# Rotating scan states out in the last phase instead of in the scan pass, with a new head for the x loads

## The chip, the cores and the metric

The kernel runs on one core of a Trainium2 chip. The metric is the device time of one execution in microseconds (us), lower is better. PE is TensorE, DVE is VectorE, ACT is ScalarE, POOL is GpSimd and SP is SyncE; SP computes nothing here and issues nearly all DMAs.

## The reference

With x of 2048 rows (time) by 1024 columns in bf16, two branches are computed and mixed by a gate per row:

```
g = sigmoid((x * gate_w).sum(-1))
a = irfft2(rfft2(x) * (w_r + 1j*w_i))                  # over both axes, to bf16

Lam = Lambda_re + 1j*Lambda_im                         # 1024 complex states
Lam_bar = exp(exp(log_dt) * Lam)
Bu[t] = x[t] @ (((Lam_bar - 1) / Lam)[:, None] * (B_re + 1j*B_im)).T
h[t] = Lam_bar * h[t-1] + Bu[t]
b[t] = 2 * real(h[t] @ (C_re + 1j*C_im).T) + x[t] * Dskip

out = g * a + (1 - g) * b
```

## The kernel before

**Scan branch.** The 1024 states are 8 blocks `jb` of 128 partitions, the 2048 times 4 chunks `c` of `TC` = 512. `pass1(jb)` does one block: PE multiplies x transposed (`xT`) with the block of B (64 matmuls, L296), ACT casts the result to `u` (L299), and DVE takes the phase out of the recurrence, so that a real scan is left: it rotates the input (`cu`, `su`, `v`, L301 to L305, by rows 0 to 2 of the table `tab`), runs two scans per chunk into `g` (L308), computes the carry to the next chunk (L313 to L317), and rotates the output into `h` (`cu`, `su`, `h`, L320 to L324, by rows 3 to 5 of `tab`). Three DVE operations of 128 x 1024 elements each do such an output rotation; it is called a trio below. `h` goes to DRAM, into `h_dram[c]` (L325). ACT and DVE build `tab` once per block (L275 to L289); its two buffers alternate.

**Fourier branch.** `gfnet()` is a generator; `pull(budget)` runs pieces of it between the passes. It transforms along columns (`fd`, matmuls L334, cast into `X` on ACT L337) and along time in two steps (L346 to L349, then, after a corner turn through DRAM, load `Bb` L434 and matmuls L440), multiplies by W on DVE (`Wr_b`, `Wi_b`, L447 to L452), and goes back the same way (L464, turn, `Cq` L485, L488, `ps_id` L506, gated into `ga` L511). `T3_sb` (`T_sb` in the profile) and `K3_sb` hold the transforms along time. Two columns of W need a repair of their own (`fixup`), for which `Wc` takes four columns of W element by element (L358 to L361).

**Phase B.** When all blocks are done, for each chunk `hch` (2 MB) is loaded from `h_dram[c]` (L542), PE multiplies it with C (`CT`, 128 matmuls a chunk, L550), and DVE forms the skip term `sk`, `pre` and the output `o` for each of four row blocks (L558, L560, L563).

**The head.** For 16 row blocks of x: load into one of three staging buffers `xn` (L157), transpose on PE, copy into `xT` (L147), and sum x times `gate_w` on DVE (`gjunk`, L159). The C blocks go through the same staging buffers later, from L265, into `CT`.

**Order.** The framework sorts the program for each engine by a cost model of its own, and each engine then runs its list strictly in order. Tiles of a pool wait for a free buffer. A DMA queue's issuing engine is held while an instruction in front of it waits.

Of the kernel before, what the change touches and what calls it, by code (L numbers as in the profile page):

```python
# [14 lines left out]
BF16 = mybir.dt.bfloat16  # L15
I32 = mybir.dt.int32
# [65 lines left out]
def kernel(  # L82
# [60 lines left out]
    def pe_transpose_block(src_ap, dst_ap, evac):  # L143
        pt = psU.tile([P, 8, P], BF16, name="pt", tag="psu")
        for j8 in range(8):
            nc.tensor.transpose(out=pt[:, j8, :], in_=src_ap[:, P * j8:P * (j8 + 1)], identity=ident)  # L146
        evac(out=dst_ap, in_=pt)  # L147

    xT = xpool.tile([P, 8, S], BF16, name="xT")
# [4 lines left out]
    gjunk = cpool.tile([P, D], BF16, name="gjunk")  # L154
    for r in range(16):
        xn = stg.tile([P, D], BF16, name="xn", tag="stg")
        nc.sync.dma_start(out=xn, in_=x[P * r:P * (r + 1), :])  # L157
        pe_transpose_block(xn, xT[:, :, P * r:P * (r + 1)], nc.vector.tensor_copy)
        nc.vector.scalar_tensor_tensor(out=gjunk, in0=xn, scalar=1.0, in1=gw_bc, op0=ALU.mult, op1=ALU.mult,  # L159
                                       accum_out=glog[:, r:r + 1])  # L160

# [94 lines left out]
    tau_i = cpool.tile([P, TC], I32, name="tau_i")  # L256
# [3 lines left out]
    CT = [ctpool.tile([P, 8, D], BF16, name=f"CT{ri}") for ri in range(2)]  # L260

    def load_CT_block(ri, q):
        src = (B_C_re, B_C_im)[ri]
        cn = stg.tile([P, D], BF16, name="cn", tag="stg")
        nc.sync.dma_start(out=cn, in_=src[P * q:P * (q + 1), :])  # L265
        pe_transpose_block(cn, CT[ri][:, :, P * q:P * (q + 1)], nc.scalar.copy)

    def pass1(jb):
        BTs = p1.tile([P, 2, 8, P], BF16, name="BTs")
        for ri, src in enumerate((B_B_re, B_B_im)):  # L270
# [16 lines left out]
        nc.scalar.mul(out=tab[:, 4, :], in_=tab[:, 3, :], mul=-1.0)  # L287
        nc.vector.scalar_tensor_tensor(out=tab[:, 5, :], in0=sn_f, scalar=ncr[:, jb:jb + 1], in1=t2,
                                       op0=ALU.mult, op1=ALU.subtract)  # L289
        rb = r_sb[:, jb:jb + 1].to_broadcast([P, TC])  # L290
        carry = None
        for c in range(NCH):
            psu = psU.tile([P, 2, TC], FP32, name="psu", tag="psu")
            for ri in range(2):
                for dblk in range(8):
                    nc.tensor.matmul(psu[:, ri, :], lhsT=BTs[:, ri, dblk, :], rhs=xT[:, dblk, TC * c:TC * (c + 1)],  # L296
                                     start=(dblk == 0), stop=(dblk == 7))
# [7 lines left out]
            nc.vector.tensor_add(out=v, in0=cu, in1=su)  # L305
            g = rp.tile([P, 2, TC], BF16, name="g")
            for ri in range(2):
                nc.vector.tensor_tensor_scan(out=g[:, ri, :], data0=rb, data1=v[:, ri, :],  # L308
                                             initial=(0.0 if carry is None else carry[:, ri:ri + 1]),
                                             op0=ALU.mult, op1=ALU.add)  # L310
# [8 lines left out]
            cg = rp.tile([P, 2, TC], BF16, name="cu")  # L319
            nc.vector.tensor_mul(out=cg, in0=g, in1=tab[:, 3:5, :])  # L320
            sg = rp.tile([P, 2, TC], BF16, name="su")
            nc.vector.tensor_mul(out=sg, in0=g[:, ::-1, :], in1=tab[:, 5:6, :].to_broadcast([P, 2, TC]))  # L322
            h = hp.tile([P, 2, TC], BF16, name="h")
            nc.vector.tensor_add(out=h, in0=cg, in1=sg)  # L324
            nc.sync.dma_start(out=h_dram[c, :, jb, :, :], in_=h)  # L325

    def gfnet():
        Acol = fx.tile([P, 16, 2], BF16, name="Acol")
# [26 lines left out]

        Wc = fx.tile([P, 16, 4], BF16, name="Wc")
        with nc.allow_non_contiguous_dma(reason="two columns of W"):
            nc.sync.dma_start(out=Wc[:, :, 0], in_=Wr_v[:, :, 0])  # L358
            nc.sync.dma_start(out=Wc[:, :, 1], in_=Wi_v[:, :, 0])  # L359
            nc.sync.dma_start(out=Wc[:, :, 2], in_=Wr_v[:, :, K])  # L360
            nc.sync.dma_start(out=Wc[:, :, 3], in_=Wi_v[:, :, K])  # L361
# [70 lines left out]
        def s2w(b):  # L432
# [95 lines left out]
    for jb in range(8):  # L528
# [2 lines left out]
            load_CT_block(*ct_blocks.pop(0))  # L531
        pull(24.0)
    pull(1e9)
    actx.close()
    with ExitStack() as bctx:
        hcp = bctx.enter_context(tc.tile_pool(name="hcp", bufs=2))
        fin = bctx.enter_context(tc.tile_pool(name="fin", bufs=2))
        psY = bctx.enter_context(tc.tile_pool(name="psY", bufs=3, space=PSUM))

        for c in range(NCH):  # L540
            hch = hcp.tile([P, 8, 2, TC], BF16, name="hch")
            nc.sync.dma_start(out=hch, in_=h_dram[c])  # L542
# [53 lines left out]
```

## Time and profile before

| | |
|---|---|
| four runs | 539.31 us median, 538.5 to 541.11 |
| profiled execution | 539.43 us, its span 537.7 us |
| mean granted TensorE clock | 0.958 |
| PE busy | 443.2 us, 82% of the span, 2343 matmuls |
| DVE busy | 355.8 us, 66% |
| ACT busy | 211.3 us, 39% |
| POOL busy | 8.3 us, 2% |
| DMA | 74.18 MB, mean 138 GB/s |

A row of the timeline gives the start, the length, the engine, the line of the kernel and the operation, output<-inputs, the shapes, how many instructions were merged, and in brackets the idle time of that engine just before, with what ended it. SPq is SP's queue of DMA instructions. A row of the stage table gives a stretch and its length, the busy time of PE, PEld (weight loads, beside PE), DVE, ACT and POOL with instruction counts, then granted clock, the DMA engines' share and GB/s. For a DMA issue the last number is the time from issue to landing.

### The profile page before, as it was taken

How to read it: one execution, taken by the hardware profiler on the slowest of the kernel's cores; microseconds unless marked ns; L12 is line 12 of the kernel's file. 1: busy time of each engine (PE TensorE's matmuls, PEld its weight loads, DVE VectorE, ACT ScalarE, POOL GpSimd, SP SyncE). 2: the span in 40 equal slices, each digit the busy share in tenths (PEclk: the TensorE clock that was granted, in tenths of full speed). 3: DMA queues.
4: the chain of work that ended last, by engine and by line, in shares of the span. 5: the costliest groups of instructions: out<-in, count | busy, mean ns of one | idle time of the engine just before them, and what ended most of it. 6: DMA issues, size and time to landing. Idle time of an engine off the chain costs nothing.

```text
span 537.7 us, 6325 instructions
## 1 busy us (share of the span) xinstructions
PE 443.2 (82%) x2343; PEld 224.9 (42%) x2343; DVE 355.8 (66%) x633; ACT 211.3 (39%) x278; POOL 8.3 (2%) x16
## 2 busy tenths in 40 slices
PE   2045998989969956899977999999890799999996
PEld 1033544544635522443433545554440344444442
DVE  4069459937940996999999990505979944444431
ACT  0000596685456345657784755653521000000000
POOL 4000000000000010000000000000000000000000
PEclk9999999899979996989998999999996699999999
DMA  9974222311412198748765343520255646555211
GB/s 205 190 175 124 54 80 77 120 59 41 125 51 79 60 208 206 212 131 265 234 195 123 126 144 119 174 102 20 99 184 206 256 135 216 176 197 195 78 40 40
DMA packets 59519, 74.18 MB, mean 138 GB/s; under 512 B 21600, under 2 KB 32096, under 8 KB 58976
## 3 DMA queue, kind: packets, MB, share of 16 engines
q1 hardware_dynamic: 54016, 69.28, 40.8%
q0 software_dynamic: 5136, 3.97, 4.8%
q10 hardware_dynamic: 336, 0.53, 0.5%
q8 instruction: 18, 0.29, 0.2%
q14 instruction: 13, 0.11, 0.1%
HBM read 52.53 MB, written 25.19 MB: 145 GB/s over the span
## 4 chain that ended last, share of the span: by engine, by line
PE 36%; DVE 34%; DMA 10%; ACT 8%; issue 6%; SPq 5%; DVEq 0%
PE ps_y L550 21%; DVE g L308 10%; PE ps_fd L334 4%; PE ps_id L506 4%; DVE cu L301 3%; DVE v L305 3%; DVE su L303 3%; DVE su L322 3%; PE psu L296 3%; DVE h L324 2%; DMA xn<-in_A_x_dram 2%; SPq L359 2%; DMA Wi_b<-in_A_w_i_dram 2%; DMA Bb<-turn_scratch 2%; DMA hch<-h_scratch 1%
## 5 line engine op out<-in xcount | busy, mean ns | idle before, releaser
L550 PE MATMUL ps_y<-CT,hch 128*128 128x512 bf16 x512 | 113.1, 385 | 15.6 <-DMA hch<-h_scratch 15.6
L296 PE MATMUL psu<-xT,BTs 128*128 128x512 bf16 x512 | 119.6, 382 | 3.2 <-ACT BTs L147 3.0
L550 PEld LDWEIGHTS <-hch 128*128 128x128 bf16 x512 | 50.5, 99 | 77.9 <-DMA hch<-h_scratch 15.7
L296 PEld LDWEIGHTS <-BTs 128*128 128x128 bf16 x512 | 49.8, 98 | 61.9 <-ACT BTs L147 4.0
L334 PE MATMUL ps_fd<-G_sb,xT 128*128 128x512 bf16 x256 | 64.8, 410 | 10.4 <-ACT X L337 9.7
L506 PE MATMUL ps_id<-Ginv_sb,ZT 128*128 128x512 bf16 x256 | 58.5, 383 | 1.7 <-ACT ga L511 1.6
L308 DVE TENSOR_TENSOR_SCAN g<-r_sb,carry,v 128x512 bf16<-128x512 f32 x48 | 59.1, 1271 | 0.5
L301 DVE TENSOR_TENSOR cu<-u,tab 128x1024 bf16<-128x1024 bf16 x32 | 22.0, 686 | 56.3 <-ACT u L299 56.1
L563 DVE SCALAR_TENSOR_TENSOR o<-ps_y,omg,pre 128x1024 bf16<-128x1024 f32 x16 | 20.5, 1284 | 57.3 <-PE ps_y L550 57.3
L334 PEld LDWEIGHTS <-xT 128*128 128x128 bf16 x256 | 37.0, 147 | 34.1 <-issue 19.1
L299 ACT CAST u<-psu 128x1024 bf16<-128x1024 f32 x32 | 32.4, 1012 | 46.7 <-PE psu L296 39.8
L146 PE MATMUL pt<-ident,xn 128*128 128x128 bf16 x128 | 16.2, 311 | 37.9 <-DMA xn<-in_A_x_dram 34.4
L506 PEld LDWEIGHTS <-ZT 128*128 128x128 bf16 x256 | 25.2, 98 | 32.6 <-issue 5.3
L159 DVE SCALAR_TENSOR_TENSOR gjunk<-xn,gw_bc 128x1024 bf16<-128x1024 bf16 x16 | 19.5, 1219 | 22.5 <-DMA xn<-in_A_x_dram 17.1
L146 PEld LDWEIGHTS <-xn 128*128 128x128 bf16 x128 | 12.5, 141 | 41.4 <-DMA xn<-in_A_x_dram 39.2
L511 ACT ACTIVATE ga<-ps_id,gA 128x1024 bf16<-128x1024 f32 x16 | 17.8, 1110 | 28.3 <-issue 14.2
L337 ACT CAST X<-ps_fd 128x1024 bf16<-128x1024 f32 x16 | 16.1, 1005 | 19.9 <-PE ps_fd L334 19.9
L305 DVE TENSOR_TENSOR v<-cu,su 128x1024 bf16<-128x1024 bf16 x32 | 22.1, 689 | 0.7
L320 DVE TENSOR_TENSOR cu<-g,tab 128x1024 bf16<-128x1024 bf16 x32 | 22.0, 687 | 0.2
L324 DVE TENSOR_TENSOR h<-cu,su 128x1024 bf16<-128x1024 bf16 x32 | 22.0, 687 | 0.2
L469 ACT CAST C<-ps_is 128x1024 bf16<-128x1024 f32 x16 | 16.3, 1017 | 14.5 <-PE ps_is L467 8.0
L303 DVE TENSOR_TENSOR su<-u,tab 128x1024 bf16<-128x1024 bf16 x32 | 21.9, 686 | 0.0
(185 smaller groups left out, 532.9 us busy)
## 6 DMA issues: line engine op xcount, KB each, us to landing
h_scratch<-h SPq DMA_DIRECT2D x32, 256.0 KB, 2.1
hch<-h_scratch SPq DMA_DIRECT2D x4, 2048.0 KB, 7.9
xn<-in_A_x_dram SPq DMA_DIRECT2D x16, 256.0 KB, 3.7
turn_scratch<-A SPq DMA_DIRECT2D x16, 256.0 KB, 3.1
Bb<-turn_scratch SPq DMA_DIRECT2D x16, 256.0 KB, 3.1
turn_scratch<-C SPq DMA_DIRECT2D x16, 256.0 KB, 3.2
Cq<-turn_scratch SPq DMA_DIRECT2D x16, 256.0 KB, 2.9
ga_scratch<-ga SPq DMA_DIRECT2D x16, 256.0 KB, 2.9
```

What stands on the lines that cost most here:

```text
L146: nc.tensor.transpose(out=pt[:, j8, :], in_=src_ap[:, P * j8:P * (j8 + 1)], identity=ident)
L296: nc.tensor.matmul(psu[:, ri, :], lhsT=BTs[:, ri, dblk, :], rhs=xT[:, dblk, TC * c:TC * (c + 1)], start=(dblk == 0), stop=(dblk == 7))
L299: nc.scalar.copy(out=u, in_=psu)
L301: nc.vector.tensor_mul(out=cu, in0=u, in1=tab[:, 0:1, :].to_broadcast([P, 2, TC]))
L303: nc.vector.tensor_mul(out=su, in0=u[:, ::-1, :], in1=tab[:, 1:3, :])
L305: nc.vector.tensor_add(out=v, in0=cu, in1=su)
L308: nc.vector.tensor_tensor_scan(out=g[:, ri, :], data0=rb, data1=v[:, ri, :], initial=(0.0 if carry is None else carry[:, ri:ri + 1]), op0= ...
L320: nc.vector.tensor_mul(out=cg, in0=g, in1=tab[:, 3:5, :])
L324: nc.vector.tensor_add(out=h, in0=cg, in1=sg)
L334: nc.tensor.matmul(ps[:, K * h:K * (h + 1)], lhsT=xT_A[:, dblk, j, :], rhs=G_sb[:, dblk, K * h:K * (h + 1)], start=(dblk == 0), stop=(dblk ...
L506: nc.tensor.matmul(psy[:, 512 * nh:512 * (nh + 1)], lhsT=ZT[:, kc, c, :], rhs=Ginv_sb[:, 4 * c + kc, 512 * nh:512 * (nh + 1)], start=(i == ...
L550: nc.tensor.matmul(psy[:, 512 * dh:512 * (dh + 1)], lhsT=hch[:, jb, ri, P * tq:P * (tq + 1)], rhs=CT[ri][:, jb, 512 * dh:512 * (dh + 1)], ...
```

## The change

It has four parts.

1. In `pass1` only chunk 0 is still rotated. Of chunks 1 to 3 the raw scan `g` goes to `h_dram`, and rows 3 to 5 of each block's table are kept in DRAM (`tab2_dram`). Phase B loads these tables (3.1 MB), and for chunk `c + 1` loads the raw states (`gch`, 2 MB) and rotates them with 8 trios while chunk `c` is multiplied.
2. Chunk 0's `hch0` has a pool of its own, so its load is issued before the pools of the first phase are released.
3. In the head the 16 x blocks are loaded straight into the `CT` tiles, which are free until then. Its other loads are moved: `dsk_bc` from ACT's queue to SP's, the four columns of `Wc` from SP's queue to POOL's, and the first quarter of `T3_sb` behind a small copy on POOL that reads the last column of `xT`.
4. Buffers: `Wr_b` and `Wi_b` three in place of two, `t1` to `t4` one, the rotation's temporaries one; `gjunk` and `tau_i` use the staging buffers, `g` shares the three buffers of `h`.

The core of the diff:

```diff
     for r in range(16):
-        xn = stg.tile([P, D], BF16, name="xn", tag="stg")
+        xn = CT[r // 8][:, r % 8, :]
         nc.sync.dma_start(out=xn, in_=x[P * r:P * (r + 1), :])
+    for r in range(16):
+        xn = CT[r // 8][:, r % 8, :]
         pe_transpose_block(xn, xT[:, :, P * r:P * (r + 1)], nc.vector.tensor_copy)
+        gjunk = stg.tile([P, D], BF16, name="gjunk", tag="stg")
...
     T3_sb = gconst.tile([P, 16, 3, P], BF16, name="T3_sb")
+    nc.gpsimd.tensor_copy(out=T3_sb[:, 0, 0, 0:1], in_=xT[:, 7, S - 1:S])
...
-            nc.sync.dma_start(out=Wc[:, :, 0], in_=Wr_v[:, :, 0])
...
+            nc.gpsimd.dma_start(out=Wc[:, :, 0], in_=Wr_v[:, :, 0])
...
+    def rotate_out(h_out, g_in, tab2):
+        cg = rp.tile([P, 2, TC], BF16, name="cu")
+        nc.vector.tensor_mul(out=cg, in0=g_in, in1=tab2[:, 0:2, :])
+        sg = rp.tile([P, 2, TC], BF16, name="su")
+        nc.vector.tensor_mul(out=sg, in0=g_in[:, ::-1, :], in1=tab2[:, 2:3, :].to_broadcast([P, 2, TC]))
+        nc.vector.tensor_add(out=h_out, in0=cg, in1=sg)
...
+        nc.sync.dma_start(out=tab2_dram[:, jb], in_=tab[:, 3:6, :])
...
-            nc.sync.dma_start(out=h_dram[c, :, jb, :, :], in_=h)
+            if c == 0:
+                h = hp.tile([P, 2, TC], BF16, name="h", tag="h")
+                rotate_out(h, g, tab[:, 3:6, :])
+                nc.sync.dma_start(out=h_dram[c, :, jb, :, :], in_=h)
+            else:
+                nc.sync.dma_start(out=h_dram[c, :, jb, :, :], in_=g)
...
+    hch0 = h0p.tile([P, 8, 2, TC], BF16, name="hch0")
+    nc.sync.dma_start(out=hch0, in_=h_dram[0])
     actx.close()
...
+        tab2 = tbp.tile([P, 8, 3, TC], BF16, name="tab2")
+        nc.sync.dma_start(out=tab2, in_=tab2_dram)
+
+        def rotated_chunk(c):
+            gch = gcp.tile([P, 8, 2, TC], BF16, name="gch")
+            nc.sync.dma_start(out=gch, in_=h_dram[c])
+            hch = hcp.tile([P, 8, 2, TC], BF16, name="hch")
+            for jb in range(8):
+                rotate_out(hch[:, jb], gch[:, jb], tab2[:, jb])
+            return hch
+
+        hch_next = hch0
         for c in range(NCH):
-            hch = hcp.tile([P, 8, 2, TC], BF16, name="hch")
-            nc.sync.dma_start(out=hch, in_=h_dram[c])
+            hch = hch_next
+            if c + 1 < NCH:
+                hch_next = rotated_chunk(c + 1)
```

How the order of the engines moves, at the three places that matter below (a row: line, operation, output<-inputs, shape, count).

SP, from its first instruction, before:

```order
L157 DMA xn<-in_A_x_dram 128x1024 x3
L165 DMA G_sb<-c_G 128x8x512 x2
L358 DMA Wc<-in_A_w_r_dram 128x16x1
L359 DMA Wc<-in_A_w_i_dram 128x16x1
L157 DMA xn<-in_A_x_dram 128x1024
L360 DMA Wc<-in_A_w_r_dram 128x16x1
L157 DMA xn<-in_A_x_dram 128x1024 x2
```

and after, where `CT_124` and `CT_125` are the two `CT` tiles:

```order
L160 DMA CT_124<-in_A_x_dram 128x1024 x8
L160 DMA CT_125<-in_A_x_dram 128x1024 x8
L171 DMA G_sb<-c_G 128x8x512 x2
L195 DMA dsk_bc<-in_B_Dskip_dram 128x1024
L448 DMA Wr_b<-in_A_w_r_dram 128x512
```

All x loads now stand first, with nothing between them, and G behind. The four `Wc` loads are on POOL, after:

```order
L182 DMA JP_sb<-c_JP 128x2x128
L370 DMA Wc<-in_A_w_r_dram 128x16x1
L371 DMA Wc<-in_A_w_i_dram 128x16x1
L372 DMA Wc<-in_A_w_r_dram 128x16x1
L373 DMA Wc<-in_A_w_i_dram 128x16x1
L264 IOTA tau_i 128x512
L173 COPY T_sb<-xT 128x1
L176 DMA T_sb<-c_T 128x4x384
```

They stand behind the other constants and ahead of the last quarter of `T_sb`.

ACT in block 2 of the passes, before, from the end of the pass on:

```order
L337 CAST X_1158<-ps_fd 128x1024
L351 CAST A_1165<-ps_s_1160 128x1024
L352 CAST Acol<-ps_s_1160 128x2
L337 CAST X_1186<-ps_fd 128x1024
L351 CAST A_1193<-ps_s_1188 128x1024
L352 CAST Acol<-ps_s_1188 128x2
L147 COPY BTs<-pt 128x1024
L280 CAST tab<-cs_f 128x512
L281 CAST tab<-sn_f 128x512
```

and after, from the same place:

```order
L292 CAST tab<-cs_f 128x512
L293 CAST tab<-sn_f 128x512
L349 CAST X_1131<-ps_fd 128x1024
L363 CAST A_1138<-ps_s_1133 128x1024
L364 CAST Acol<-ps_s_1133 128x2
L150 COPY BTs<-pt 128x1024
```

The two table casts, which need a table buffer that DVE has finished with, moved ahead of the casts of `X`.

DVE at the first chunk of the last pass, before:

```order
L558 TENSOR_TENSOR sk<-xc,dsk_bc 128x1024
L301 TENSOR_TENSOR cu<-u,tab 128x1024
L303 TENSOR_TENSOR su<-u,tab 128x1024
L560 SCALAR_TENSOR_TENSOR pre<-sk,omg,gac 128x1024
L305 TENSOR_TENSOR v<-cu,su 128x1024
L558 TENSOR_TENSOR sk<-xc,dsk_bc 128x1024
L308 SCALAR_TENSOR_TENSOR g<-r_sb,v 128x512 x2
L560 SCALAR_TENSOR_TENSOR pre<-sk,omg,gac 128x1024
```

and after, at the end of that pass, with its last scans (first row) and the start of the rotation of chunk 1 (`tab_3804` is `tab2`):

```order
L321 SCALAR_TENSOR_TENSOR g<-r_sb,carry,v 128x512 x2
L275 TENSOR_TENSOR cu<-gch,tab_3804 128x1024
L277 TENSOR_TENSOR su<-gch,tab_3804 128x1024
L588 TENSOR_TENSOR sk<-xc,dsk_bc 128x1024
L278 TENSOR_TENSOR hch<-cu,su 128x1024
L590 SCALAR_TENSOR_TENSOR pre<-sk,omg,gac 128x1024
L275 TENSOR_TENSOR cu<-gch,tab_3804 128x1024
L277 TENSOR_TENSOR su<-gch,tab_3804 128x1024
L593 SCALAR_TENSOR_TENSOR o<-ps_y,omg,pre 128x1024
```

The work of `sk` and `pre` left the last pass and stands between the trios of chunk 1, and the first output `o` of chunk 0 between them as well.

More of the change, by code (lines that the diff above doesn't have):

```diff
@@ L117 @@
     h_dram = dram.tile([NCH, P, 8, 2, TC], BF16, name="h_scratch")
+    tab2_dram = dram.tile([P, 8, 3, TC], BF16, name="tab2_scratch")
     g_dram = dram.tile([S], FP32, name="g_scratch")
@@ L123 @@
     ctpool = ctx.enter_context(tc.tile_pool(name="ctpool", bufs=1))
+    h0p = ctx.enter_context(tc.tile_pool(name="h0p", bufs=1))
     actx = ExitStack()
@@ L127 @@
     gt = actx.enter_context(tc.tile_pool(name="gt", bufs=3))
-    wp = actx.enter_context(tc.tile_pool(name="wp", bufs=2))
+    wp = actx.enter_context(tc.tile_pool(name="wp", bufs=3))
+    wt = actx.enter_context(tc.tile_pool(name="wt", bufs=1))
     fx = actx.enter_context(tc.tile_pool(name="fx", bufs=1))
@@ L132 @@
     up = actx.enter_context(tc.tile_pool(name="up", bufs=3))
-    rp = actx.enter_context(tc.tile_pool(name="rp", bufs=2))
+    rp = actx.enter_context(tc.tile_pool(name="rp", bufs=1))
     hp = actx.enter_context(tc.tile_pool(name="hp", bufs=3))
@@ L147, in pe_transpose_block @@
         evac(out=dst_ap, in_=pt)
+    CT = [ctpool.tile([P, 8, D], BF16, name=f"CT{ri}") for ri in range(2)]
     xT = xpool.tile([P, 8, S], BF16, name="xT")
@@ L153 @@
     glog = cpool.tile([P, 16], FP32, name="glog")
-    gjunk = cpool.tile([P, D], BF16, name="gjunk")
     for r in range(16):
-        xn = stg.tile([P, D], BF16, name="xn", tag="stg")
+        xn = CT[r // 8][:, r % 8, :]
         nc.sync.dma_start(out=xn, in_=x[P * r:P * (r + 1), :])
+    for r in range(16):
+        xn = CT[r // 8][:, r % 8, :]
         pe_transpose_block(xn, xT[:, :, P * r:P * (r + 1)], nc.vector.tensor_copy)
+        gjunk = stg.tile([P, D], BF16, name="gjunk", tag="stg")
         nc.vector.scalar_tensor_tensor(out=gjunk, in0=xn, scalar=1.0, in1=gw_bc, op0=ALU.mult, op1=ALU.mult,
@@ L187 @@
     dsk_bc = cpool.tile([P, D], BF16, name="dsk_bc")
-    nc.scalar.dma_start(out=dsk_bc, in_=B_Dskip.partition_broadcast(P))
+    nc.sync.dma_start(out=dsk_bc, in_=B_Dskip.partition_broadcast(P))
     Wr_v = A_w_r.rearrange("(p b) k -> p b k", b=16)
@@ L254 @@
     ncr = sp.tile([P, 8], FP32, name="ncr"); nc.vector.tensor_scalar_mul(out=ncr, in0=cr, scalar1=-1.0)
-    tau_i = cpool.tile([P, TC], I32, name="tau_i")
+    tau_i = stg.tile([P, TC], I32, name="tau_i", tag="stg")
     nc.gpsimd.iota(tau_i, pattern=[[1, TC]], base=0, channel_multiplier=0)
     tau_f = cpool.tile([P, TC], FP32, name="tau_f"); nc.vector.tensor_copy(out=tau_f, in_=tau_i)
-    CT = [ctpool.tile([P, 8, D], BF16, name=f"CT{ri}") for ri in range(2)]
     def load_CT_block(ri, q):
@@ L305, in pass1 @@
             nc.vector.tensor_add(out=v, in0=cu, in1=su)
-            g = rp.tile([P, 2, TC], BF16, name="g")
+            g = hp.tile([P, 2, TC], BF16, name="g", tag="h")
             for ri in range(2):
@@ L318, in pass1 @@
                                                in1=k1[:, 1:2], op0=ALU.mult, op1=ALU.add)
[L319 to L324, printed above, removed]
-            nc.sync.dma_start(out=h_dram[c, :, jb, :, :], in_=h)
+            if c == 0:
[4 more added lines that the diff above has]
+                nc.sync.dma_start(out=h_dram[c, :, jb, :, :], in_=g)
     def gfnet():
@@ L357, in gfnet @@
         with nc.allow_non_contiguous_dma(reason="two columns of W"):
[L358 to L361, printed above, removed]
+            nc.gpsimd.dma_start(out=Wc[:, :, 0], in_=Wr_v[:, :, 0])
+            nc.gpsimd.dma_start(out=Wc[:, :, 1], in_=Wi_v[:, :, 0])
+            nc.gpsimd.dma_start(out=Wc[:, :, 2], in_=Wr_v[:, :, K])
+            nc.gpsimd.dma_start(out=Wc[:, :, 3], in_=Wi_v[:, :, K])
         nc.sync.dma_start(out=col0_dram, in_=Acol)
@@ L446, in s2w @@
             X3 = gt.tile([P, 2, K], BF16, name="X3", tag="gx3")
-            t1 = wp.tile([P, K], BF16, name="t1"); nc.vector.tensor_mul(out=t1, in0=Wr_b, in1=X2[:, 0, :])
-            t2 = wp.tile([P, K], BF16, name="t2"); nc.vector.tensor_mul(out=t2, in0=Wi_b, in1=X2[:, 1, :])
+            t1 = wt.tile([P, K], BF16, name="t1"); nc.vector.tensor_mul(out=t1, in0=Wr_b, in1=X2[:, 0, :])
+            t2 = wt.tile([P, K], BF16, name="t2"); nc.vector.tensor_mul(out=t2, in0=Wi_b, in1=X2[:, 1, :])
             nc.vector.tensor_sub(out=X3[:, 0, :], in0=t1, in1=t2)
-            t3 = wp.tile([P, K], BF16, name="t3"); nc.vector.tensor_mul(out=t3, in0=Wr_b, in1=X2[:, 1, :])
-            t4 = wp.tile([P, K], BF16, name="t4"); nc.vector.tensor_mul(out=t4, in0=Wi_b, in1=X2[:, 0, :])
+            t3 = wt.tile([P, K], BF16, name="t3"); nc.vector.tensor_mul(out=t3, in0=Wr_b, in1=X2[:, 1, :])
+            t4 = wt.tile([P, K], BF16, name="t4"); nc.vector.tensor_mul(out=t4, in0=Wi_b, in1=X2[:, 0, :])
             nc.vector.tensor_add(out=X3[:, 1, :], in0=t3, in1=t4)
@@ L533 @@
     pull(1e9)
+    hch0 = h0p.tile([P, 8, 2, TC], BF16, name="hch0")
+    nc.sync.dma_start(out=hch0, in_=h_dram[0])
     actx.close()
     with ExitStack() as bctx:
+        tbp = bctx.enter_context(tc.tile_pool(name="tbp", bufs=1))
         hcp = bctx.enter_context(tc.tile_pool(name="hcp", bufs=2))
+        gcp = bctx.enter_context(tc.tile_pool(name="gcp", bufs=2))
+        rp = bctx.enter_context(tc.tile_pool(name="rp2", bufs=1))
         fin = bctx.enter_context(tc.tile_pool(name="fin", bufs=2))
         psY = bctx.enter_context(tc.tile_pool(name="psY", bufs=3, space=PSUM))
+        tab2 = tbp.tile([P, 8, 3, TC], BF16, name="tab2")
[8 more added lines that the diff above has]
+        hch_next = hch0
         for c in range(NCH):
-            hch = hcp.tile([P, 8, 2, TC], BF16, name="hch")
-            nc.sync.dma_start(out=hch, in_=h_dram[c])
+            hch = hch_next
+            if c + 1 < NCH:
+                hch_next = rotated_chunk(c + 1)
             for tq in range(4):
```

## The prediction

> **What bounds the kernel now.** I read the page's chain that ended last first, then a table of engine time by stage, cut where the chain changes its engine, and then the timeline at the cuts. The chain by engine:
>
> ```profile
> PE 36%; DVE 34%; DMA 10%; ACT 8%; issue 6%; SPq 5%; DVEq 0%
> ```
>
> The chain is shared about equally by PE and DVE, so an average says little. By stage (length; busy PE, PEld, DVE, ACT, POOL; granted clock; DMA share; GB/s):
>
> ```profile
> 0.00:54.90 54.90, 16.34 (x132) 12.62 (x132) 27.95 (x48) 1.28 (x1) 6.51 (x14) 1.00 0.79 173
> 54.90:192.10 137.20, 125.87 (x625) 68.87 (x626) 92.58 (x179) 88.73 (x138) 1.78 (x2) 0.96 0.24 75
> 192.10:206.70 14.60, 5.33 (x24) 2.34 (x25) 14.14 (x21) 4.55 (x7) 0.00 (x0) 0.75 1.18 255
> 206.70:290.60 83.90, 72.78 (x439) 33.39 (x439) 78.09 (x195) 55.03 (x63) 0.00 (x0) 0.96 0.64 189
> 290.60:388.60 98.00, 94.82 (x534) 50.10 (x535) 59.47 (x98) 54.97 (x64) 0.00 (x0) 0.98 0.36 119
> 388.60:419.90 31.30, 15.03 (x81) 7.18 (x82) 27.54 (x41) 6.70 (x7) 0.00 (x0) 0.80 0.59 201
> 419.90:537.70 117.80, 113.05 (x512) 50.44 (x512) 56.00 (x57) 0.00 (x0) 0.00 (x0) 0.98 0.41 143
> ```
>
> PE is full in the second, fifth and last stage; DVE in the fourth (78.09 of 83.90) and sixth; nobody in the first. The rotation that leaves pass 1 is 24 trios, and where PE is full its absence is worth nothing. The run shown took 539.43 us for a span of 537.7, so 1.7 us lie around it; the median of the runs is 539.31.
>
> **The head, 0 to 54.9.** From the timeline (start, length, engine, line, then idle before and its cause):
>
> ```profile
> 6.19 1.23 DVE L159 SCALAR_TENSOR_TENSOR gjunk<-xn,gw_bc 128x1024 bf16<-128x1024 bf16 x1 [5.32 <-DMA gw_bc<-in_gate_w_dram]
> 7.24 6.80 SPq L358 DMA_DIRECT2D Wc<-in_A_w_r_dram  x1
> 7.45 1.22 DVE L159 SCALAR_TENSOR_TENSOR gjunk<-xn,gw_bc 128x1024 bf16<-128x1024 bf16 x1
> ...
> 9.87 1.28 DVE L147 COPY xT<-pt 128x1024 bf16<-128x1024 bf16 x2
> 14.08 9.84 SPq L359 DMA_DIRECT2D Wc<-in_A_w_i_dram  x1
> 28.53 1.23 DVE L159 SCALAR_TENSOR_TENSOR gjunk<-xn,gw_bc 128x1024 bf16<-128x1024 bf16 x1 [16.18 <-DMA xn<-in_A_x_dram]
> 54.15 0.69 DVE L147 COPY xT<-pt 128x1024 bf16<-128x1024 bf16 x1 [0.27 <-PE pt L146]
> 54.90 1.50 PE L334 MATMUL ps_fd<-G_sb,xT 128*128 128x512 bf16 x3 [0.62 <-DVE xT L147]
> ```
>
> SP spends 6.80 + 9.84 us issuing two column gathers of W while the fourth x load stands behind them, and DVE waits 16.18 us for it; later x loads wait in turn for a free staging buffer. After the change SP's first rows are all 16 x loads, the gathers are POOL's, and the first fd matmul waits for the sixteenth copy into xT. DVE's own work until then is 15 gate products at 1.27 (7.45 less 6.19, with the accumulator read) and 16 copies at 0.68 (between 0.64, half of the pair above, and 0.69): 19.1 + 10.9 = 30.0 us from 6.19, or 36.2. The x bytes hide under that: 4.2 MB of x and some 1.9 MB of constants on POOL's queue, at the 255 GB/s of the third stage, are in at about 24 us, and 2.1 MB of G behind them at about 32. I allow 0.8 us for small gaps and take 37.0, that is **−17.9**. Bounds: −19 (DVE without a gap), −10 (DMA decides, a rival below).
>
> The cover of the gathers is thin, though. They now stand fifth to eighth on POOL's queue, and DVE's cast of Wc stands ahead of the whole setup of angles and gates, which ACT needs for the second X. The rows that price it (issue to landing; then q1's packets, MB and share within 28 to 30 us, when little but such 2-byte packets moved):
>
> ```profile
> JP_sb<-c_JP POOLq DMA_DIRECT2D x1, 64.0 KB, 18.4
> Wc<-in_A_w_r_dram SPq DMA_DIRECT2D x1, 4.0 KB, 5.0
> Wc<-in_A_w_i_dram SPq DMA_DIRECT2D x1, 4.0 KB, 13.7
> q1 hardware_dynamic: 1358, 0.04, 46.0%
> ```
>
> JP, the last constant ahead of them, was issued at 6.1 and so landed at 24.5. Four gathers have 4 × 2048 packets; at 1358 in 2 us that is 12.1 us, so 36.6. One after the other at 5.0 us it would be 44.5, at 13.7 us 79. DVE wants them at about 37.5. I take 36.6, hidden, since a queue of transfers does not pay the landing of each; 44.5 would cost up to 7 us.
>
> T's first quarter is held behind the copy that reads xT, and then behind the gathers in the same queue. Its first reader (first and last start):
>
> ```profile
> L346 PE MATMUL ps_s<-X,T_sb x16: 377/380/380, 64.1 to 189.0; 128*128 128x512 bf16 x16
> ```
>
> That is 9.2 us after the first fd matmul, so at 46 now, and a quarter issued at 37 behind a drained queue should be in by 43 to 45. Cost 0; if late, it adds to the same bound.
>
> The Trainium skill, page "DMA: Bandwidth & Descriptors", sections "Issuing engine by pattern" and "Issuing engines are not separate DMA queues", speaks against the move to GpSimd: simple transfers belong on Sync, whose hardware path is generally faster, and another issuing engine saves only the sequencer's time, "usually small relative to the DMA itself". By that the head would keep nearly all of its 17 us and the kernel end near 535. The trace differs on "small": the issue itself held SP for 16.64 us, with x loads behind it.
>
> **Stage 1, 54.9 to 206.7, bound by PE.** The rows that carry it:
>
> ```profile
> 92.54 5.30 PE L334 MATMUL ps_fd<-G_sb,xT 128*128 128x512 bf16 x16 [2.02 <-ACT X L337]
> 98.94 3.61 PE L334 MATMUL ps_fd<-G_sb,xT 128*128 128x512 bf16 x16
> 150.03 0.62 ACT L280 CAST tab<-cs_f 128x512 bf16<-128x512 f32 x1 [4.71 <-DVE su L322]
> 153.17 4.43 PE L334 MATMUL ps_fd<-G_sb,xT 128*128 128x512 bf16 x10 [4.93 <-ACT X L337]
> 206.71 0.58 PE L440 MATMUL ps_s<-Bb,K_sb 128*128 128x512 bf16 x1 [9.28 <-DMA Bb<-turn_scratch]
> ```
>
> The first stall (2.02, and 1.69 for the slower matmuls behind it: 5.30 against 3.61) is of a busy ACT in block 0, whose order is relaxed now: I take −3.5, between −3.7 and 0. The second comes from ACT waiting for a table buffer that the previous pass's DVE work still reads. Dropping three trios frees DVE sooner, but the order puts the table casts ahead of X a block earlier, so the wait moves and stays: 0 (−5 to +3). The third, 9.28, runs through the last turn write and the first Bb load. One X stands behind the moved table casts there: +1.5 (0 to +4). The eight writes of table rows (384 KB each) fall where the DMA share is 0.24 to 0.64: 0.
>
> **Stages 206.7 to 388.6.** The first is DVE's. Three trios of the block in flight leave it, 5.4 us (9 ops at 0.60 start to start, priced below); but the scans of the next block's second chunk, 4.4 us, now stand ahead of the last X3. The third W buffer saves under 1 us. I take 0 (−5.5 to +3). The second has PE busy 94.82 of 98.00: 0 (−3 to 0).
>
> **Last pass and phase B.** Timeline rows:
>
> ```profile
> 388.56 3.63 PE L296 MATMUL psu<-xT,BTs 128*128 128x512 bf16 x16 [1.22 <-ACT BTs L147]
> 398.39 0.69 DVE L558 TENSOR_TENSOR sk<-xc,dsk_bc 128x1024 bf16<-128x1024 bf16 x1 [3.51 <-DMA xc<-in_A_x_dram]
> ...
> 400.20 1.28 DVE L560 SCALAR_TENSOR_TENSOR pre<-sk,omg,gac 128x1024 f32<-128x1024 bf16 x1
> ...
> 401.40 0.68 DVE L305 TENSOR_TENSOR v<-cu,su 128x1024 bf16<-128x1024 bf16 x1
> ...
> 411.24 2.46 DVE L308 TENSOR_TENSOR_SCAN g<-r_sb,carry,v 128x512 bf16<-128x512 f32 x2
> 411.99 0.33 SPq L542 DMA_DIRECT2D hch<-h_scratch  x1
> 417.98 2.46 DVE L308 TENSOR_TENSOR_SCAN g<-r_sb,carry,v 128x512 bf16<-128x512 f32 x2
> 419.88 10.34 PE L550 MATMUL ps_y<-CT,hch 128*128 128x512 bf16 x36 [15.57 <-DMA hch<-h_scratch]
> 532.99 1.28 DVE L563 SCALAR_TENSOR_TENSOR o<-ps_y,omg,pre 128x1024 bf16<-128x1024 f32 x1 [5.62 <-PE ps_y L550]
> ```
>
> In before's coordinates the last psu still starts at 388.56. Its first chunk's rotation is no longer held by sk and pre, which waited for xc until 398.39: h comes at about 400, hch0 lands after the 3.1 MB of tables and its own 7.9 us (411.99 to 419.88), at about 412.5, 7.4 earlier. That does not reach the end of the kernel, because the second chunk needs DVE. Three such DVE ops (sk and two of the input rotation) run from 398.39 to 400.20, 0.60 each start to start, so a trio is 1.81; pre is 1.20. Scan chunks stood 6.74 us apart (411.24 to 417.98); without the trio 4.93, so the last scan ends near 414.8, its write and gch (7.9) at 423.2. Until the eighth slice of chunk 1 the order puts on DVE 24 rotation ops at 0.60 (14.5 us), 6 sk at 0.60, 5 pre at 1.20, 4 o at 1.28: 29.2 us, so 452.4. PE has 128 matmuls per chunk at 0.221 (113.1 us for 512): chunk 0 ends at 440.8, and 32 matmuls of chunk 1 don't need the eighth slice, to 447.8. So PE stalls 4.6 us and loses 1.5 more to a slow clock (as the 1.69 above). Then 96 matmuls, 21.2, end chunk 1 at 475.1; chunk 2's rotation (23.3 us of DVE) and chunk 3's fit beside 28.3 us of matmuls. The end is 475.1 + 56.5 = 531.6 against 533.0: **−1.4**. Bounds: −7.4 (no stall), +5.7 (PE fills nothing: 452.4 + 84.8 + 1.5 = 538.7).
>
> **Sum.** −17.9 − 3.5 + 1.5 + 0 + 0 − 1.4 = −21.3: span 516.4, time 518.1, so 518 (−3.9%).
>
> **Rivals.**
> (a) The head is bound by the 16 DMA engines. For: they were busy 0.79 of 54.9 us, 43.4 us of work, and moving the issue leaves the 8192 small packets on them. Against: part of these 43.4 us was W, B and C blocks that fd does not need. fd then starts at 44.4, −10.5 instead of −17.9: 525.7. Chance 0.12.
> (b) Phase B becomes DVE's and PE cannot fill, the +5.7 above: 525.2. For: DVE's 56.00 us there gain 72 ops, 43.4 us, and 99.4 of 117.8 leaves little; against: only chunk 1 has a late start. Chance 0.15.
> (c) All the rotation was on the path: 24 × 1.81 = 43.4 in place of the small terms, 539.4 − 43.4 − 17.9 = 478. Against: PE's three full stages. Chance 0.04.
> (d) Slower: the gathers land late on POOL's queue and hold DVE's setup. At 13.7 us each they land from 24.5 at 79; from 37.5 on each microsecond costs at most one. It decides once they land 21 us late, at 59 or later; at 64 the kernel takes 544. Chance 0.05. At some 58 it ends within 0.5% of before: 0.04.
>
> **How the numbers follow.** My forecast has 0.60, (a) 0.12, (b) 0.15, (c) 0.04, (d) 0.05, no change 0.04. About 0.5% (2.7 us) is what a measurement can tell here. Faster: 0.60 + 0.12 + 0.15 + 0.04 = 0.91. The low end takes the head's −19, stage 1's −5 and DVE's −5.5 in the fourth stage: 507. The high end has (a) or (b) with 4 us for the turn: 530.
>
> **What would show it.** Right: fd starts near 37; no DVE wait over 2 us for x; a PE wait of about 5 us for hch in chunk 1, with none in chunks 2 and 3. Wrong: a DVE wait at the cast of Wc, a PE wait for T at the first stage-1 matmul, PE waits for hch in every chunk, or a stall above 12 us at Bb.

## The result and the profile after

| kernel | median us | range, runs | profiled execution: time, span, clock |
|---|---|---|---|
| before | 539.77 | 536.97 to 541.11, 15 | 539.43, 537.7, 0.958 |
| after | 517.64 | 516.14 to 519.53, 11 | 519.53, 517.7, 0.945 |

The ratio is 0.9602, 95% interval [0.9584, 0.962]. The forecast was 518. The profiled execution is the slowest of the eleven, 1.9 us above the median, so 19.9 us of difference stand in the two traces for 22.1 in the medians.

The stages of the changed kernel, cut at the same events as before (columns as in the stage table of before):

```profile
0.00:34.90 34.90, 13.34 (x132) 11.88 (x132) 27.32 (x48) 1.28 (x1) 10.35 (x17) 0.89 1.06 229
34.90:189.80 154.90, 134.74 (x655) 72.37 (x656) 90.23 (x173) 94.59 (x146) 3.65 (x4) 0.93 0.41 115
189.80:272.80 83.00, 71.66 (x431) 32.98 (x431) 78.85 (x196) 53.71 (x61) 0.00 (x0) 0.95 0.66 198
272.80:370.00 97.20, 95.18 (x536) 50.56 (x536) 41.42 (x66) 54.90 (x64) 0.00 (x0) 0.98 0.38 123
370.00:391.90 21.90, 15.04 (x80) 7.21 (x80) 17.24 (x28) 6.79 (x7) 0.00 (x0) 0.94 0.83 313
391.90:517.70 125.80, 116.31 (x512) 50.70 (x512) 96.20 (x126) 0.00 (x0) 0.00 (x0) 0.95 0.46 155
```

Stage by stage that is −20.0 (head), +3.1 (54.90 to 206.71 was 151.8), −0.9, −0.8, −9.4 (last pass) and +8.0 (phase B). In these two traces the head's gain equals the whole; what the last pass gains, phase B gives back. DVE goes from 56.00 us in phase B to 96.20. The page's chain, which was followed back only to 369.99 us here and so covers just the last pass and phase B, has DVE as its largest engine:

```profile
DVE 15%; PE 6%; issue 4%; DMA 2%; ACT 0%; DVEq 0%; SPq 0%
```

The head in the timeline of the changed kernel:

```profile
0.74 15.51 SPq L160 DMA_DIRECT2D CT<-in_A_x_dram  x16
...
16.02 1.28 DVE L150 COPY xT<-pt 128x1024 bf16<-128x1024 bf16 x2
...
17.22 1.22 DVE L165 SCALAR_TENSOR_TENSOR gjunk<-CT,gw_bc 128x1024 bf16<-128x1024 bf16 x1
...
18.36 1.28 DVE L150 COPY xT<-pt 128x1024 bf16<-128x1024 bf16 x2
...
34.90 10.05 PE L346 MATMUL ps_fd<-G_sb,xT 128*128 128x512 bf16 x32 [1.53 <-DVE xT L150]
...
36.31 0.78 POOL L176 DMA_DIRECT2D T_sb<-c_T  x1 [0.30 <-POOL T_sb L173]
...
36.45 0.19 DVE L400 CAST Wc_f<-Wc 128x64 f32<-128x64 bf16 x1
```

SP has all x loads issued by 16.3 us, DVE goes on without a gap from there, and the cast of Wc waits for nothing. Stage 1 keeps its stalls of PE, and phase B has the forecast stall for `hch` in chunk 1, in two pieces, after DVE idled 8.95 us for the raw chunk:

```profile
81.01 5.30 PE L346 MATMUL ps_fd<-G_sb,xT 128*128 128x512 bf16 x16 [2.27 <-ACT X L349]
124.29 6.25 PE L346 MATMUL ps_fd<-G_sb,xT 128*128 128x512 bf16 x16 [4.27 <-ACT X L349]
173.61 0.38 PE L358 MATMUL ps_s<-X,T_sb 128*128 128x512 bf16 x1 [3.52 <-ACT X L349]
189.79 0.59 PE L452 MATMUL ps_s<-Bb,K_sb 128*128 128x512 bf16 x1 [6.69 <-DMA Bb<-turn_scratch]
391.93 31.90 PE L580 MATMUL ps_y<-CT,hch 128*128 128x512 bf16 x138 [6.14 <-DMA hch<-h_scratch]
426.52 2.69 PE L580 MATMUL ps_y<-CT,hch 128*128 128x512 bf16 x6 [2.69 <-DVE hch L278]
430.12 29.42 PE L580 MATMUL ps_y<-CT,hch 128*128 128x512 bf16 x128 [0.91 <-DVE hch L278]
```

```profile
404.56 0.69 DVE L275 TENSOR_TENSOR cu<-gch,tab 128x1024 bf16<-128x1024 bf16 x1 [8.95 <-DMA gch<-h_scratch]
513.17 1.28 DVE L593 SCALAR_TENSOR_TENSOR o<-ps_y,omg,pre 128x1024 bf16<-128x1024 f32 x1 [5.62 <-PE ps_y L580]
```

### The profile page after: what moved, and what is told of

It is laid out like the page before. It is cut to its first block, busy times and chain, and to the rows that moved or that the text cites. A ratio compares the mean times of both kernels' runs of the same rounds, so it can differ in the third digit from the quotient of the medians.

```text
span 517.7 us, 6351 instructions
## 1 busy us (share of the span) xinstructions
PE 446.3 (86%) x2343; PEld 225.7 (44%) x2343; DVE 351.3 (68%) x633; ACT 211.3 (41%) x278; POOL 14.0 (3%) x21
## 5 line engine op out<-in xcount | busy, mean ns | idle before, releaser
L580 PE MATMUL ps_y<-CT,hch 128*128 128x512 bf16 x512 | 116.3, 390 | 11.0 <-DMA hch<-h_scratch 6.1
L309 PE MATMUL psu<-xT,BTs 128*128 128x512 bf16 x512 | 121.5, 384 | 1.2 <-ACT BTs L150 1.2
L523 ACT ACTIVATE ga<-ps_id,gA 128x1024 bf16<-128x1024 f32 x16 | 17.8, 1114 | 30.5 <-issue 21.0
L149 PE MATMUL pt<-ident,CT 128*128 128x128 bf16 x128 | 13.1, 281 | 19.6 <-DVE xT L150 13.3
L165 DVE SCALAR_TENSOR_TENSOR gjunk<-CT,gw_bc 128x1024 bf16<-128x1024 bf16 x16 | 19.4, 1219 | 6.8 <-DMA gw_bc<-in_gate_w_dram 5.6
L275 DVE TENSOR_TENSOR cu<-gch,tab 128x1024 bf16<-128x1024 bf16 x24 | 16.5, 688 | 9.1 <-DMA gch<-h_scratch 8.9
L316 DVE TENSOR_TENSOR su<-u,tab 128x1024 bf16<-128x1024 bf16 x32 | 21.9, 686 | 0.0
L457 ACT CAST X<-ps_s 128x1024 bf16<-128x1024 f32 x16 | 16.3, 1020 | 12.5 <-PE ps_s L455 12.5
L149 PEld LDWEIGHTS <-CT 128*128 128x128 bf16 x128 | 11.6, 131 | 20.8 <-issue 13.5
```

The lines of the kernel that those rows point to most:

```text
L275: nc.vector.tensor_mul(out=cg, in0=g_in, in1=tab2[:, 0:2, :])
L580: nc.tensor.matmul(psy[:, 512 * dh:512 * (dh + 1)], lhsT=hch[:, jb, ri, P * tq:P * (tq + 1)], rhs=CT[ri][:, jb, 512 * dh:512 * (dh + 1)], ...
```

## Experiments

The theory at the start: the head is the whole gain, by 16 x loads with nothing ahead of them; the deferred rotation nets zero, because phase B is paced by DVE's path over raw chunk 1. Rivals: the deferral earns or costs by itself; in the head, SP's issue of the gathers, or the three staging buffers, was the cause.

### The two halves

**Head alone.** The edit, on the kernel before, is the head's part of the diff (x into `CT`, Wc on POOL's queue, T's first quarter held, `dsk_bc` on SP).

> The kernel before with the new head alone (x blocks straight into the CT tiles, Wc on POOL's queue, the first quarter of T held back, dsk_bc on SP); rotation and buffers as before. Theory (the head is the whole gain, the deferred rotation is worth nothing in sum): first fd matmul at 34 to 36 us, time 518 to 522. Rival A (the deferral earns part of it, for instance by the 9 us earlier start of the last phase): 525 to 531. Rival B (the deferral costs, because DVE paces the last phase): 510 to 515.

Measured: 522.31 (521.69 to 525.2), ratio 0.9704 [0.9674, 0.9734], first fd matmul at 34.76. Just above the theory's range; a wait for T that the changed kernel does not show stands in its timeline:

```profile
47.90 0.38 PE L349 MATMUL ps_s<-X,T_sb 128*128 128x512 bf16 x1 [4.43 <-DMA T_sb<-c_T]
```

**Deferral alone.** The changed kernel with the old head (`gjunk` in one of the rotation's buffers, for space).

> The changed kernel with the head of before (three staging buffers, Wc on SP between the x loads). Theory (deferral nets zero): first fd matmul at 54 to 56 us, time 537 to 541; the last phase starts some 9 us earlier than before and ends about where it ended. Rival A (deferral earns): 526 to 533. Rival B (deferral costs): 543 to 548.

Measured: 537.6 (536.77 to 539.62), ratio 0.9977 [0.996, 0.9994], fd at 55.16. PE starts phase B at 412.66 (419.88 before) and the last `o` at 532.97 (532.99 before). So on the old head the deferral nets −1.2 us, about the bound of what can be told here: the theory holds there, and 7 us at the start of phase B came back as nothing at its end:

```profile
412.66 12.69 PE L578 MATMUL ps_y<-CT,hch 128*128 128x512 bf16 x50 [6.41 <-DMA hch<-h_scratch]
...
532.97 1.28 DVE L591 SCALAR_TENSOR_TENSOR o<-ps_y,omg,pre 128x1024 bf16<-128x1024 f32 x1 [5.62 <-PE ps_y L578]
```

The two halves do not add up to the whole. By their ratios they give 16.0 and 1.2 us, 17.2 together, and the whole change gives 21.5. The 4.43 us for T in e1 is of the missing size, but it need not be all of it: e10 below (x loads alone) has no such wait and still lies 3.2 us above the changed kernel, with an interval that begins at 0.9642 where the changed kernel's ends at 0.962. So with the new head the deferral, or the moves that e10 leaves out, are worth some 3 us. The traces do not show which step earns them: the two spans differ by 1.0 us (518.7 and 517.7), e10's being its fastest execution and the changed kernel's its slowest.

### What in the head

**Gathers back on SP.**

```diff
-            nc.gpsimd.dma_start(out=Wc[:, :, 0], in_=Wr_v[:, :, 0])
+            nc.sync.dma_start(out=Wc[:, :, 0], in_=Wr_v[:, :, 0])
...
```

> The changed kernel with the four Wc gathers back on SP's queue, where they stand behind all x loads and G. Theory (what mattered is that nothing stands ahead of the x loads, not which queue issues the gathers): first fd matmul at 35 us still; the gathers' 17 us of issue now hold W and B blocks, and the cast of Wc in DVE's setup waits for them until 42 to 48, so 519 to 526. Rival (moving the gathers off SP was itself the gain): the head goes back by more than 10 us, 528 to 536.

Measured: 518.51 (516.79 to 520.73), ratio 0.9636 [0.961, 0.9663], fd at 34.70. Behind the x loads the gathers on SP cost nothing that can be told from the changed kernel.

**Only the gathers moved.** The same edit the other way round, on the kernel before.

> The kernel before with the Wc gathers alone moved to POOL's queue; x goes on through three staging buffers, with G between. Theory (SP's issue of the gathers was most of the head's loss, and the rest is G ahead of the fourth x load): first fd matmul at 39 to 45 us, time 524 to 531. Rival (three staging buffers pace the head whatever SP does): fd at 50 or later, 534 to 540.

Measured: 540.39 (538.8 to 543.76), ratio 1.0028 [1.0007, 1.005], fd at 55.27. The theory fell. The timeline shows why:

```profile
6.08 1.01 SPq L165 DMA_DIRECT2D G_sb<-c_G  x2
7.13 7.36 SPq L436 DMA_DIRECT2D Wr_b<-in_A_w_r_dram  x1
...
15.49 0.79 SPq L157 DMA_DIRECT2D xn<-in_A_x_dram  x1
...
30.61 1.23 DVE L159 SCALAR_TENSOR_TENSOR gjunk<-xn,gw_bc 128x1024 bf16<-128x1024 bf16 x1 [18.36 <-DMA xn<-in_A_x_dram]
```

SP issues the fourth x load 8.6 us earlier than before (24.05 there) and it lands 2 us later. With the gathers gone, the next load is held 7.36 us instead, and x then lies behind G's 2 MB, the constants and the gathers' packets. The trace of before had shown already that a gather need not be long in issue: its third and fourth took 0.55 us each, the third here:

```profile
25.45 0.55 SPq L360 DMA_DIRECT2D Wc<-in_A_w_r_dram  x1
```

**Direct x loads alone.**

```diff
-        xn = stg.tile([P, D], BF16, name="xn", tag="stg")
+        xn = CT[r // 8][:, r % 8, :]
```

> The kernel before with one part of the new head: x goes straight into the CT tiles. Wc stays on SP, T's first quarter and dsk_bc stay where they were. Theory (all of the head's gain is that the x loads stand first): first fd matmul at 34 to 38 us, and no 4.4 us wait for T as in e1: 517 to 523. Rival (holding T back and moving the gathers are needed, or x queues behind them): fd at 40 or later, 525 to 532.

Measured: 520.84 (520.53 to 522.63), ratio 0.9668 [0.9642, 0.9694], fd at 35.95:

```profile
35.95 8.81 PE L336 MATMUL ps_fd<-G_sb,xT 128*128 128x512 bf16 x32 [1.54 <-DVE xT L147]
```

So one of the head's four moves has nearly all of its gain; holding T, moving the gathers and moving `dsk_bc` are not needed for it.

**G held back**, with three staging buffers and the gathers on POOL.

```diff
+    nc.gpsimd.tensor_copy(out=G_sb[:, 0, 0:1], in_=xT[:, 7, P * 12 - 1:P * 12])
+    nc.gpsimd.tensor_copy(out=G_sb[:, 0, K:K + 1], in_=xT[:, 7, P * 12 - 1:P * 12])
     cG_v = cG.rearrange("(j p) k -> p j k", p=P)
```

> e4 (three staging buffers, Wc on POOL's queue) with G held back until twelve x blocks are copied, so that nothing large stands ahead of the fourth x load. Theory (what delayed x was the 2 MB of G and the gathers' packets ahead of it, not the three buffers): no DVE wait over 6 us for x, first fd matmul at 40 to 46, 525 to 532. Rival (three buffers pace the head): fd at 50 or later, 535 to 541.

Measured: 534.49 (533.61 to 535.51), ratio 0.9913 [0.9884, 0.9943], fd at 48.93, between the two. The fourth block is now at DVE at 16.79, in e4 at 30.61, so most of its wait of 18.36 was G ahead of it. The load of `Wr_b` that SP was held on for 7.36 us in e4 is issued in 0.33: the holds are no fixed cost of one DMA, and those seen here stand behind G. But the seventh block still waits:

```profile
6.10 0.33 SPq L438 DMA_DIRECT2D Wr_b<-in_A_w_r_dram  x1
...
16.74 1.03 PE L146 MATMUL pt<-ident,xn 128*128 128x128 bf16 x8 [5.20 <-DMA xn<-in_A_x_dram]
...
27.32 1.03 PE L146 MATMUL pt<-ident,xn 128*128 128x128 bf16 x8 [7.07 <-DMA xn<-in_A_x_dram]
...
46.25 1.89 PE L146 MATMUL pt<-ident,xn 128*128 128x128 bf16 x16 [4.30 <-DMA xn<-in_A_x_dram]
```

Three buffers allow three loads ahead, each issued when DVE frees a buffer, and each then moves beside the other traffic. Of the 20 us, holding G gave 6.3 (55.27 to 48.93). Part of the rest belongs to this edit itself: the last two x loads stand behind the first half of G on SP (40.66, after 40.17), and PE waits 4.30 us for them. What is left goes with loads that could not be issued ahead of time, as e10 issues them.

**T not held back.**

```diff
-    nc.gpsimd.tensor_copy(out=T3_sb[:, 0, 0, 0:1], in_=xT[:, 7, S - 1:S])
```

> The changed kernel without the copy that holds T's first quarter back. Theory (T is 0.4 MB of some 8 ahead of fd, and DVE paces the head): first fd matmul within 1 us of 34.9, 516 to 519. Rival (the hold pays, because DMA paces the head): fd 1.5 us or more later, 519 to 522.

Measured: 518.95 (517.58 to 521.25), ratio 0.963 [0.9597, 0.9663]. The first fd matmul comes at 36.81, 1.9 us later, as the rival said, and what it waits for is G:

```profile
36.81 10.02 PE L345 MATMUL ps_fd<-G_sb,xT 128*128 128x512 bf16 x32 [3.57 <-DMA G_sb<-c_G]
```

In the times the interval holds the changed kernel's ratio, so the 1.9 us at fd is seen and its worth at the end is not.

### What in phase B and stage 1

**No early load of chunk 0.** `hch0` comes from phase B's own pool.

> The changed kernel with chunk 0 loaded from the last phase's own pool, so that its load may wait for memory. Theory (the last phase is paced by DVE's rotation of chunk 1, and PE's start has some 3 us of slack there): 516 to 520 even if the first matmul comes 1 to 3 us later. Rival (the early load of chunk 0 pays): 521 or more.

Measured: 518.13 (516.57 to 518.73), ratio 0.9596 [0.9561, 0.9632]. PE's first `ps_y` is 22.2 us after the start of the last pass (390.97 less 368.78), 21.9 in the changed kernel. The load was hardly later, so this shows that the pool of its own is not needed; it does not test the slack.

**Two chunks deferred.**

```diff
-            if c == 0:
+            if c < 2:
...
+            if c == 0:
+                hch_next = hcp.tile([P, 8, 2, TC], BF16, name="hch")
+                nc.sync.dma_start(out=hch_next, in_=h_dram[1])
+            elif c + 1 < NCH:
```

> The changed kernel with only chunks 2 and 3 deferred: chunk 1 is rotated in the scan passes again. Theory (the last phase is late by DVE's path over the wait for raw chunk 1 and its 8 trios): no PE wait for hch after the first, the last matmul some 114 us after the first, and most of the 8 trios hidden where PE is full: 510 to 515. Rival (the passes are bound by DVE, so 8 more trios of 1.8 us cost what they save): 517 to 525.

Measured: 513.69 (513.2 to 516.53), ratio 0.9534 [0.9498, 0.9571], below the changed kernel's interval. Its groups of phase B, against the changed kernel's (busy, mean ns, then idle before by cause; some of its matmul records are missing):

```profile
L583 PE MATMUL ps_y<-CT,hch 128*128 128x512 bf16 x502 | 112.7, 385 | 8.5 <-DMA hch<-h_scratch 8.0
```

```profile
L580 PE MATMUL ps_y<-CT,hch 128*128 128x512 bf16 x512 | 116.3, 390 | 11.0 <-DMA hch<-h_scratch 6.1 <-DVE hch L278 4.9
```

PE has no wait for DVE, and phase B from the first matmul to the last `o` takes 113.2 us (393.59 to 506.83) against 121.2 (391.93 to 513.17). The last pass grows by 2.3 us. DVE's path in chunk 1 was what gave the time back.

**Raw chunks in two pieces.**

```diff
-            nc.sync.dma_start(out=gch, in_=h_dram[c])
+            nc.sync.dma_start(out=gch[:, 0:7], in_=h_dram[c, :, 0:7])
+            nc.sync.dma_start(out=gch[:, 7:8], in_=h_dram[c, :, 7:8])
```

> The changed kernel with each raw chunk loaded in two pieces, blocks 0 to 6 and block 7, so that the first piece need not wait for the last scan. Theory (DVE's 8.9 us idle before the rotation of chunk 1 is the load's wait for the last pass): DVE starts to rotate at about 398 to 400 in place of 404.6 and the kernel ends 3 to 6 us earlier, 511 to 515. Rival (memory for the raw chunk is free only when the passes end): first trio at 404 to 405, 516 to 519.

Measured: 514.22 (512.91 to 517.64), ratio 0.9543 [0.9497, 0.9589]. The interval just reaches the changed kernel's. DVE idles 4.65 us in place of 8.95 between its last scan and the rotation. PE's wait moves one chunk on and shrinks:

```profile
397.92 0.69 DVE L275 TENSOR_TENSOR cu<-gch,tab 128x1024 bf16<-128x1024 bf16 x1 [4.65 <-DMA h_scratch<-g]
...
454.15 52.64 PE L581 MATMUL ps_y<-CT,hch 128*128 128x512 bf16 x237 [3.59 <-DVE hch L278]
```

**Both, for chunk 0.** e6 with `hch0` in two pieces.

```diff
-    nc.sync.dma_start(out=hch0, in_=h_dram[0])
+    nc.sync.dma_start(out=hch0[:, 0:7], in_=h_dram[0, :, 0:7])
+    nc.sync.dma_start(out=hch0[:, 7:8], in_=h_dram[0, :, 7:8])
```

> e6 (only chunks 2 and 3 deferred) with chunk 0's early load in two pieces, blocks 0 to 6 and block 7. Theory (with DVE off the path, the last phase is PE's 113 us plus PE's wait of 8 us for the 2 MB of chunk 0): the last pass's piece is 256 KB and lands in 2 to 3 us, PE starts 4 to 7 us earlier than in e6 against the start of the last pass, 507 to 511. Rival (PE's order needs block 7 at once, or the small piece queues behind the 3.1 MB of tables): within 2 us of e6, 512 to 516.

Measured: 514.49 (513.03 to 515.25), ratio 0.954 [0.9514, 0.9565]: the same as e6. PE does start 6.4 us earlier, 17.8 us after the start of the last pass (371.12) in place of 24.2, but then:

```profile
388.94 20.88 PE L584 MATMUL ps_y<-CT,hch 128*128 128x512 bf16 x96 [1.10 <-ACT CT L150]
415.11 15.19 PE L584 MATMUL ps_y<-CT,hch 128*128 128x512 bf16 x56 [5.28 <-DVE o L597]
```

```profile
409.56 0.69 DVE L275 TENSOR_TENSOR cu<-gch,tab 128x1024 bf16<-128x1024 bf16 x1 [10.50 <-DMA gch<-h_scratch]
...
413.78 1.28 DVE L597 SCALAR_TENSOR_TENSOR o<-ps_y,omg,pre 128x1024 bf16<-128x1024 f32 x1
```

Three row blocks of results fill the three PSUM buffers, and the `o` that would free one stands in DVE's list behind the first trio of chunk 2, which waits 10.50 us for its load. The theory's step to PE's start held, the time did not; neither side named this wait.

**Three table buffers**, on e5.

```diff
+    ptab = actx.enter_context(tc.tile_pool(name="ptab", bufs=3))
...
-        tab = p1.tile([P, 6, TC], BF16, name="tab")
+        tab = ptab.tile([P, 6, TC], BF16, name="tab")
```

> e5 with three table buffers in place of two. Theory (the stalls of 4.3 and 3.5 us in stage 1 are ACT waiting for a table buffer ahead of its casts of X): both stalls gone with the slow matmuls behind them, 8 to 11 us less than e5 in stage 1, some of it lost at the turn: 508 to 514. Rival (the casts of X are late for another reason, or PE's gain ends at the turn's DMA): within 2 us of e5.

Measured: 516.0 (513.31 to 517.29), ratio 0.956 [0.9522, 0.9598], 2.1 us under e5 with intervals that overlap. The theory's 8 to 11 us did not come. ACT's casts of `tab` around the waits:

```profile
96.67 0.63 ACT L292 CAST tab<-cs_f 128x512 bf16<-128x512 f32 x1
121.44 0.62 ACT L292 CAST tab<-cs_f 128x512 bf16<-128x512 f32 x1 [2.06 <-DVE su L316]
167.30 0.62 ACT L292 CAST tab<-cs_f 128x512 bf16<-128x512 f32 x1 [5.28 <-DVE su L316]
```

The cast at 96.67 is the fourth; in the changed kernel the fourth is the one at 122.19 that waits. The scheduler used the third buffer to make tables one block further ahead, so the fifth waits for the DVE pass that the fourth waited for. Whether the stall would go if the table casts stood behind those of X was not tried.

## Why the prediction was right, point by point

- **Head, −17.9; measured −20.0.** The size held: DVE paces it, and its last copy decides. The copies cost 0.60 each start to start (16.02 to 17.22 for two, in place of 0.68) and a gate product 1.14 between them (17.22 to 18.36, in place of 1.27). **The cause given was wrong.** The step "SP spends 6.80 + 9.84 us issuing two column gathers of W while the fourth x load stands behind them" put the loss on the issue of the gathers; e4 takes it away and gains nothing, and before's other two gathers took 0.55 each. The three buffers and the bytes ahead did it (e10, e12). There the sentence from the Trainium skill, "DMA: Bandwidth & Descriptors", "Issuing engines are not separate DMA queues", that I weighed against the trace, was the better guide: by it moving the gathers saves sequencer time alone, and e3 and e4 agree (the changed kernel with them back on SP 518.51, its interval overlapping; the kernel before with them alone on POOL 540.39). Its consequence for this kernel, "end near 535", did not follow, since the new head also orders the x loads.
- **Gathers and T hidden, 0.** Right here: no wait at the cast of Wc (36.45), T used at 44.79 without a wait. The cover of T is thin as said: in e1 it was late by 4.43.
- **Stage 1, −3.5, with +1.5 for the turn; measured +3.1.** The term −3.5 failed: the stall of block 0 stands, 2.27 with the same 5.30 us behind it, where 2.02 and 5.30 were; the order of ACT still has angle and table work ahead of that X, and ACT waits 2.18 us there for a table operation of DVE. Nor do the slow matmuls counted in that term follow from the stall alone: behind stalls of 2.04 (e1) and 2.03 (e10) the same 16 took 3.61. The stall that "moves and stays" did (4.27 for 4.93). At the turn 3.52 and 6.69 stand for the 9.28 of before, +0.9. About 0.7 us more is a slower first pair of fd groups (10.05 for 32 matmuls, 9.37 before). Over the whole stage PE's idle time hardly changed (20.2 us, 20.6 before); its busy time rose from 131.20 (649 matmuls) to 134.74 (655), which the forecast had no term for. Other kernels with the same deferral take 152.5 (e3) to 154.2 us (e2) for this stage, and e10 without it 152.1, so part of the +3.1 belongs to the one execution that was profiled.
- **Stages 206.7 to 388.6, 0 and 0; measured −0.9 and −0.8.**
- **Last pass and phase B, −1.4; measured −1.3** (143.1 from the last psu to the last `o`, 144.4 before). PE began at 410.4 in before's coordinates (412.5 forecast). The stall in chunk 1 was 3.6 (2.69 and 0.91; 4.6 forecast), and 0.29 and 1.00 followed in chunks 2 and 3, where none was forecast. The eighth slice came when forecast (452.2 in before's coordinates, 452.4 forecast), but PE waited for the sixth and the seventh and not for it. Matmul time rose by 3.2, more than the 1.5 allowed for slow matmuls. So DVE's path was right, and that the sum came within 0.1 is partly luck: the earlier start and the shorter stall were lost again to matmul time and the later waits.
- **Rivals.** (a) did not come: the first fd matmul waited for DVE, and 8.0 MB moved in its 34.9 us at 229 GB/s, where 9.5 MB had moved in 54.9 at 173. DMA is close behind, though: in e1, e7 and e8 the same matmul waited last for G (1.65 to 1.77 us). (The 525.7 of this rival should be 525.5 by its own terms.) (b) came only as the forecast's own stall. (c) is excluded by the result, and by e2, where moving the 24 trios nets 1.2 us. (d) did not come: the cast of Wc ran at 36.45 without a wait, and the gathers, landing 17.8 to 21.7 us after their issues at 6.06 to 14.88, overlapped.

Two misses partly cancelled, the head 2.1 better and stage 1 with its turn 5.1 worse; the median, not the profiled execution, hit 518, and that it came so close is partly luck.

## What to carry to other kernels

When many small loads pass through a few staging buffers, look at which bytes lie ahead of each load and when it may be issued, before blaming the engine that issues them; memory that is needed only later served as staging here at no cost that the runs show. Work moved out of one stage is worth only what the later stage can hide of it, so move no more than that: here two chunks in place of three gained 4 us more. An engine's in-order list makes one late operand hold up work that others wait for (e9), and a third buffer can be spent by the scheduler on running further ahead (e7).

## What the runs showed that was not expected

Executions of one kernel differ by as much as some of the effects above. The changed kernel's two at a mean granted clock of 0.945 took 519.25 and 519.53, its nine at 0.949 to 0.955 took 516.14 to 518.71; e5 took 518.73 at 0.945 and 516.57 at 0.958, e11 521.25 and 517.58. So in these three kernels some 2 to 3 us go with the lowest clock. It is no rule: e1 took 521.69 and 525.2 at the same 0.947, and e10 520.93 at 0.947 and 520.53 at 0.963. Why the clock differs was not tested. The first 32 fd matmuls, the same work, took 8.72 (e1), 9.37 (before) and 10.05 (after). Ahead of them PE is idle for long, up to 8.59 us at a time in the changed kernel; whether that sets their pace is not shown:

```profile
16.76 1.86 PE L149 MATMUL pt<-ident,CT 128*128 128x128 bf16 x16 [8.59 <-DVE xT L150]
```

A single profile of a kernel can thus be off by as much as the smaller effects here.
